# Transformer block with sliding-window attention on one core: dense matmuls in four column tiles, reordered score columns, an earlier output weight

## The chip, the cores and the metric

The kernel runs on one core of one Trainium2 chip. The metric is device time in microseconds (us) of one execution, the median over several runs. Names of engines: PE is TensorE (matmuls), DVE is VectorE, ACT is ScalarE, POOL is GpSimd, SP is SyncE, which here only issues DMA transfers.

## The reference

One layer with two branches on the same normalised input: attention with 32 heads of 20 dimensions over 2048 positions, each query seeing the last 256 keys, and a gated feed-forward part. All inputs are bf16.

```python
B, S, D = 1, 2048, 640          # F = 1536
xn = _layernorm(x)

# A: sliding-window attention, H = 32, Dh = 20, W = 256
q, k, v = split_heads(xn @ wqkv)
scores = einsum("bhqd,bhkd->bhqk", q, k) * Dh ** -0.5
mask = (idx[:, None] - idx[None, :] >= 0) & (idx[:, None] - idx[None, :] < W)
p = softmax(where(mask, scores, -1e9))
a = einsum("bhqk,bhkd->bhqd", p, v).reshape(B, S, D) @ wo

# B: gated feed-forward
b = (sigmoid(xn @ w_gate) * (xn @ w_up)) @ w_down

out = x + a + b
```

## The kernel before

The 2048 positions are cut into four chunks of 512 (`CW`), and a chunk into four blocks of 128. For each chunk there are these pieces of work.

- Layer norm of the chunk, and its transposed form `xnT`. Chunk 0 is transposed on PE (L276), chunks 1 to 3 by DMA transposes that SP issues (`turn_block`, L280).
- The q and k projections (`proj_block`, L296): 128 weight columns per matmul, taken from `wqkv` with a step of five, 512 columns of `xnT` streamed, five matmuls to sum over 640. Results go to bf16 on DVE (q) and ACT (k), to a scratch tensor in DRAM, and back as `qT` and `kT` (`spread`, L311) in a layout where each group of four heads stands at partitions 0, 32, 64 and 96.
- The v projection (`project_v`, L322): `xnT` as weights, 320 columns streamed. A column of 0.5 beside each head's v gives the softmax denominator.
- Gate and up (`g_gu`, L396 and L403): 24 times five matmuls of 512 columns per chunk. ACT takes tanh (L399), DVE makes `h` (L407).
- Down (`down`, L417) and the attention output (`add_wo`, L424), both into the same PSUM tile `y`, in halves of 320 columns; DVE adds x (L428), SP stores.

All these are called dense below. Their matmuls have 128 by 128 weights and fill the whole array.

The attention itself runs in steps over groups of four heads (`HG`); there are eight groups. A step (`wide_step`, `full_step`) computes 512 columns of scores per head, in units of 64 queries by 64 keys. Keys stand on the partitions in two halves (`hf`) of 64, and the four heads of a group use four row bands of the array: the score matmuls (L463) have weights of 20 rows by 64 columns. Chunk 0 has 16 wide steps; each later chunk has 16 wide steps (two per group) and four full steps (one per pair of groups, for blocks that no mask cuts). Each step writes the one PSUM tile `ps` (four banks, one buffer); ACT takes the exp into `pT` (L469, four buffers), in two instructions; POOL then clears what the mask forbids (L473): units on the diagonal (`diag`), the oldest unit (`oldest`), and a shifted copy of a unit that holds two half-forbidden ones (`late`), one instruction per place.

Two steps after a group's last step, PV for it is issued (`pv`, L494): for each head v's 32 columns as weights, at column band 32i of the array, so the four heads' matmuls go to four tiles of 32 columns. Its result `acc` is transposed and scaled on DVE into `oc`.

The order on PE is the program's order. The loop at the end walks over all 76 steps: PV of a group that is due, then the step's scores, then a share of dense work, pulled from a list of generators (`fill.add`, L643 to L661). Each generator yields its estimated PE time, and the loop spreads what is left up to the next due point evenly over the steps, by `units` (8 in every step). Transfers stand in the same list, so their place in it fixes their place in SP's queue, which is worked through in order. The last chunk's down and output are written out by hand after the loop, with the last PV among them.

The output weight `wo` has to be rearranged by heads: `turn_wo` (L220) copies it within DRAM to `wo_i`, and `load_wo` (L225) loads that. Its first use is in `out0`, the output of chunk 0. `load_wd` (L216) loads the down weights.

Of the kernel before, what the change touches and what calls it, by code (L numbers as in the profile page):

```python
# [9 lines left out]
P = 128  # L10
S = 2048
D = 640
# [3 lines left out]
DC = D // P  # L16
FC = F // P
CW = 512
NCH = S // CW
SBC = CW // P  # L20
HG = 4
# [3 lines left out]
HALF = 320  # L25
FS = 768
EPS = 1e-5
SCALE = DH ** -0.5
# [5 lines left out]
GE = mybir.AluOpType.is_ge  # L34
BF16 = mybir.dt.bfloat16
FP32 = mybir.dt.float32
EXP = mybir.ActivationFunctionType.Exp
# [5 lines left out]
U = 64  # L43
# [10 lines left out]

def wide_step(g, r, old):

    q = 2 * r  # L60
    scores = [(g, 0, r, q, 5, 0)]
    if old:
        scores += [(g, 1, r, q + 1, 5, 1), (g, 1, r - 2, q + 1, 1, 0), (g, 0, r + 2, q + 4, 2, 5),
                   (g, 1, r + 2, q + 5, 1, 6), (g, 1, r - 2, q, 1, 7), (g, 0, r - 2, q, 1, 7)]
        return dict(scores=scores, exps=[(0, 5, 0), (5, 3, 6)], late=[(0, 9), (6, 5)], diag=[0, 6],
                    oldest=[4, 8], pv=[(g, r, q, 6, 0), (g, r + 2, q + 4, 2, 6), (g, r - 2, q, 2, 8)],
                    units=8)

    scores += [(g, 1, r, q, 6, 0)]
    if r == 0:  # L70
        scores += [(g, 0, 2, 4, 3, 5), (g, 1, 2, 5, 2, 6)]
        last = [(g, 2, 4, 3, 6)]
    else:
        scores += [(g, 0, 3, 6, 2, 5), (g, 1, 3, 7, 1, 6), (g, 0, 2, 7, 1, 7), (g, 1, 2, 7, 1, 7)]
        last = [(g, 3, 6, 2, 6), (g, 2, 7, 1, 8)]
    return dict(scores=scores, exps=[(0, 5, 0), (5, 3, 6)], late=[(6, 5)], diag=[0, 6], oldest=[4],
                pv=[(g, r, q, 6, 0)] + last, units=8)


def full_step(gs):  # L80

    out = dict(scores=[], exps=[], late=[], diag=[], oldest=[], pv=[], units=8)
    for n, g in enumerate(gs):
        out["exps"].append((4 * n, 4, 4 * n))
        for r, q, col in ((-1, 0, 4 * n), (2, 6, 4 * n + 2)):
            out["scores"] += [(g, hf, r, q, 2, col) for hf in range(2)]
            out["pv"].append((g, r, q, 2, col))
    return out


def steps_of(c):
# [20 lines left out]
def kernel(  # L112
# [169 lines left out]
    def new_xnT(c):  # L282
        xnT[c] = xtp.tile([P, DC, CW], BF16, name="xnT")


    qk = {}
    vt = {}

    def proj_block(w, c, m):


        base = 0 if w == "q" else D
        ps = ps_d.tile([P, CW], FP32, name="pqk", tag="d")
        for d in range(DC):
            wt = wqkv[:, d, base:base + D].rearrange("p (k m) -> p m k", m=DC)
            nc.tensor.matmul(ps, lhsT=wt[:, m, :], rhs=xnT[c][:, d, :],  # L296
                             start=(d == 0), stop=(d == DC - 1))
        st = stp.tile([P, CW], BF16, name="st")
        if w == "q":
            nc.vector.tensor_copy(out=st, in_=ps)  # L300
        else:
            nc.scalar.copy(out=st, in_=ps)
        dst = scratch[w, c % 2].rearrange("(h j) s -> h j s", j=32)
        nc.sync.dma_start(out=dst[:, 4 * m:4 * m + 4, :], in_=st)
# [14 lines left out]
    def project_v(c, s, hf):  # L319
        ps = ps_d.tile([P, CW], FP32, name="pv", tag="d")  # L320
        for d in range(DC):
            nc.tensor.matmul(ps[:, 0:HALF], lhsT=xnT[c][:, d, s * P:(s + 1) * P],  # L322
                             rhs=wqkv[:, d, 2 * D + hf * HALF:2 * D + (hf + 1) * HALF],
                             start=(d == 0), stop=(d == DC - 1))
        return ps

    def copy_v(c, s, hf, ps, copy):
# [60 lines left out]
    def part(w, d, f):  # L388
        k, first = divmod(f * P, FS)
        return w[k][:, d, first:first + P]  # L390

    def g_gu(c, f0, f1):
        for f in range(f0, f1):
            pg = ps_d.tile([P, CW], FP32, name="pg", tag="d")
            for d in range(DC):
                nc.tensor.matmul(pg, lhsT=part(wg, d, f), rhs=xnT[c][:, d, :],  # L396
                                 start=(d == 0), stop=(d == DC - 1))
            th = tp.tile([P, CW], FP32, name="th")
            nc.scalar.activation(out=th, in_=pg, func=TANH, scale=0.5)  # L399
            yield 5 * MM  # L400
            pu = ps_d.tile([P, CW], FP32, name="pu", tag="d")
            for d in range(DC):
                nc.tensor.matmul(pu, lhsT=part(wu, d, f), rhs=xnT[c][:, d, :],  # L403
                                 start=(d == 0), stop=(d == DC - 1))
            h = hp.tile([P, CW], BF16, name="h")
            ht[c, f] = h
            nc.vector.scalar_tensor_tensor(out=h, in0=th, scalar=1.0, in1=pu, op0=ADD, op1=MULT)  # L407
            yield 5 * MM
# [5 lines left out]

    def down(c, s, y, cut):
        for f in range(FC):
            nc.tensor.matmul(y[:, 0:cut[1] - cut[0]], lhsT=ht[c, f][:, s * P:(s + 1) * P],  # L417
                             rhs=wd[:, f, cut[0]:cut[1]], start=(f == 0), stop=False)
            if f % 6 == 5:
                yield 6 * 136  # L420

    def add_wo(c, s, y, cut):
        for m in range(DC):
            nc.tensor.matmul(y[:, 0:cut[1] - cut[0]], lhsT=oc[c, m][:, s * P:(s + 1) * P],  # L424
                             rhs=wo[:, m, cut[0]:cut[1]], start=False, stop=(m == DC - 1))

    def add_x(c, s, y, cut, rows):
        nc.vector.scalar_tensor_tensor(  # L428
# [27 lines left out]
    def scores(c, step):  # L456
        pt = pp.tile([P, HG, PTW], BF16, name="pT")
        ps = ps_s.tile([P, HG, CW], FP32, name="ps")
        for g, hf, r, q, n, col in step["scores"]:
            kc, kb = divmod(c * SBC + r, SBC)  # L460
            key = kb * P + hf * U
            for i in range(HG):
                nc.tensor.matmul(  # L463
                    ps[hf * U:(hf + 1) * U, i, col * U:(col + n) * U],
                    lhsT=qk["k", kc][32 * i:32 * i + DH, g, key:key + U],
                    rhs=qk["q", c][32 * i:32 * i + DH, g, q * U:(q + n) * U],
                    start=True, stop=True)
        for col, n, to in step["exps"]:
            nc.scalar.activation(out=pt[:, :, to * U:(to + n) * U], in_=ps[:, :, col * U:(col + n) * U],  # L469
                                 func=EXP, scale=SCALE)  # L470

        def keep(out, in_, pattern, base, sign):
            nc.gpsimd.affine_select(out=out, in_=in_, pattern=[[0, HG], [sign, pattern]], compare_op=GE,  # L473
                                    fill=0.0, base=base, channel_multiplier=-sign)

        def cols(u, n):
            return pt[:, :, u * U:u * U + n]

        for a, b in step["late"]:
            keep(cols(b, U), cols(a, U), U, -1 - U, -1)  # L480
        for u in step["oldest"]:
            keep(cols(u, U), cols(u, U), U, -1, -1)
        for u in step["diag"]:
            keep(cols(u, P), cols(u, P), P, 0, 1)
        return pt

    def pv(c, g, parts):
# [76 lines left out]
    def mix(a, b, first, every=1, rest=True):  # L564

        for k, cost in enumerate(a):
            yield cost
            if k >= first and (k - first) % every == 0:
                yield next(b, 0)
        if rest:  # L570
            yield from b
# [66 lines left out]
    def later(load, *args):  # L638
        load(*args)
        yield 0  # L640

    norms2 = g_norms(2, True)
    fill.add("gu0", mix(g_gu(0, 0, 12), g_norms(1, True), 9), 12 * GU)  # L643
    fill.add("x2", later(load_x, 2), 0)
    fill.add("wd", later(load_wd), 0)
    fill.add("qk1", g_qk(1), 50 * MM)
    fill.add("v1", g_v(1), 40 * 136)
    fill.add("wo_i", later(turn_wo), 0)
    fill.add("gu1a", mix(g_gu(1, 0, 2), norms2, 0, 2, False), 2 * GU)
    fill.add("wo", later(load_wo), 0)  # L650
    fill.add("out0", mix(g_out(0), norms2, 0, 2), OUT)
    fill.add("x3", later(load_x, 3), 0)
    fill.add("qk2", g_qk(2), 50 * MM)
# [21 lines left out]
    for t, (c, k, step) in enumerate(todo):  # L675
        if k == 0 and c > 0:
            fill.until(f"qk{c}")
        if k == 2 and c > 0:
            fill.until(f"v{c}")
        for group in [x for x in ends if ends[x] == t - 2]:  # L680
            fill.flush()
            pv(*group, parts.pop(group))
            if group[1] == NG - 1:
                fill.shut.discard(f"out{group[0]}")
        made = (step, scores(c, step))
        for g in dict.fromkeys(piece[0] for piece in step["pv"]):
            parts.setdefault((c, g), []).append(made)
        last, label = next(x for x in cuts if t < x[0])
        credit += fill.left(label) * step["units"] / sum(x[2]["units"] for x in todo[t:last])
        credit = fill.pull(credit)  # L690
    fill.pull(10 ** 9)
    fill.flush()
# [61 lines left out]
```

## Time and profile before

| | |
|---|---|
| median of 13 runs | 317.22 us (316.85 to 319.74) |
| profiled execution | 317.37 us, of which the profile's span is 315.4 |
| PE busy | 306.9 us (97%) |
| ACT busy | 198.1 us (63%) |
| POOL busy | 178.9 us (57%) |
| DVE busy | 154.3 us (49%) |
| granted PE clock | full, in all slices |
| DMA | 33.05 MB, mean 105 GB/s, busiest in the first 80 us |

The profile is one execution. A row of its groups names the source line, the engine, the operation, the tiles (written from read) and the shapes, then the busy time, the mean duration of one in ns, and the idle time of the engine just before such instructions with what ended it. Matmuls overlap, so their mean duration is longer than the distance from one start to the next, and a busy PE need not be streaming at its full rate. The timeline merges neighbouring instructions of a kind and gives the start and length of the whole.

### The profile page before, as it was taken

The page shows a single profiled execution, that of the slowest core. Times are in us where ns is not written, and L with a number is a line of the kernel's source. Part 1 is how long each engine was busy: PE and PEld are TensorE (multiplying, and loading weights), DVE is VectorE, ACT ScalarE, POOL GpSimd, SP SyncE. Part 2 cuts the span into 40 slices and gives each one's busy share as a digit, 9 for nine tenths or more (in the row PEclk, how much of TensorE's full clock was granted, in tenths as well). Part 3 has the DMA queues.
Part 4 walks back from the last instruction along what each step waited for, and adds up shares of the span by engine and source line. Part 5 has one row for each costly group of instructions (what it writes and reads, how often), then busy time and mean ns, then how long its engine had stood idle before and what let it go on. Part 6 is the DMA issues. An engine that isn't in the chain of part 4 may idle for free.

```text
span 315.4 us, 10274 instructions
## 1 busy us (share of the span) xinstructions
PE 306.9 (97%) x4370; PEld 175.4 (56%) x4410; DVE 154.3 (49%) x313; ACT 198.1 (63%) x255; POOL 178.9 (57%) x417
## 2 busy tenths in 40 slices
PE   8999999999989999999999999999999999999996
PEld 3654444456556655544466655544456664444674
DVE  3531486654854563347753542444552433563234
ACT  5723887788845458677744457776765657878200
POOL 3000487667768548565975647476365767676300
PEclk9999999999999999999999999999999999999999
DMA  7985958836754255510036025600000010000002
GB/s 255 375 302 191 323 194 133 295 94 208 257 94 61 52 173 176 148 51 2 0 43 88 23 89 144 224 3 2 3 3 23 25 42 3 2 2 2 0 2 83
DMA packets 34572, 33.05 MB, mean 105 GB/s; under 512 B 9920, under 2 KB 33984, under 8 KB 34496
## 3 DMA queue, kind: packets, MB, share of 16 engines
q1 hardware_dynamic: 34096, 32.14, 34.6%
q8 instruction: 34, 0.56, 0.7%
q10 hardware_dynamic: 432, 0.28, 0.3%
q14 instruction: 10, 0.08, 0.1%
HBM read 21.00 MB, written 10.26 MB: 99 GB/s over the span
## 4 chain that ended last, share of the span: by engine, by line
PE 88%; DMA 6%; ACT 3%; issue 2%; SPq 1%; DVE 0%; ACTq 0%
PE pg L396 16%; PE pu L403 16%; PE y L417 14%; PE pqk L296 13%; PE ps L463 8%; PE acc L494 7%; PE y L424 6%; PE pv L322 5%; DMA wo_i<-in_A_wo_dram 2%; PE d L417 2%; DMA sk<-st 2%; ACT pT L469 1%; DMA wo<-wo_i 1%; DMA xc<-in_A_x_dram 1%; SPq L220 1%
## 5 line engine op out<-in xcount | busy, mean ns | idle before, releaser
L473 POOL TENSOR_SCALAR_AFFINE_SELECT pT<-pT 128x256 bf16<-128x256 bf16 (+1 forms) x352 | 164.8, 502 | 114.8 <-ACT pT L469 114.5
L469 ACT ACTIVATE pT<-ps 128x1280 bf16<-128x1280 f32 (+2 forms) x152 | 147.4, 1023 | 64.8 <-PE ps L463 61.7
L407 DVE SCALAR_TENSOR_TENSOR h<-th,pu 128x512 bf16<-128x512 f32 x48 | 32.8, 683 | 56.6 <-PE pu L403 33.2
L396 PE MATMUL pg<-xnT,wg 128*128 128x512 bf16 x222 | 58.7, 380 | 0.9
L403 PE MATMUL pu<-xnT,wu 128*128 128x512 bf16 x228 | 58.0, 380 | 1.1 <-issue 0.6
L417 PE MATMUL y<-wd,h 128*128 128x320 bf16 (+1 forms) x348 | 50.2, 297 | 0.0
L296 PE MATMUL pqk<-xnT,wqkv 128*128 128x512 bf16 x190 | 45.5, 382 | 0.5
L417 PEld LDWEIGHTS <-h 128*128 128x128 bf16 x396 | 36.7, 98 | 14.1 <-issue 0.2
L504 DVE STREAM_TRANSPOSE t<-acc 128x512 f32<-128x512 f32 x32 | 22.8, 712 | 33.5 <-PE acc L494 33.3
L399 ACT ACTIVATE th<-pg 128x512 f32<-128x512 f32 x48 | 28.8, 601 | 14.4 <-PE pg L396 7.7
L403 PEld LDWEIGHTS <-wu 128*128 128x128 bf16 x240 | 22.0, 98 | 25.4 <-issue 0.6
L396 PEld LDWEIGHTS <-wg 128*128 128x128 bf16 x240 | 22.0, 98 | 24.8 <-issue 0.4
L463 PEld LDWEIGHTS <-kT 20*64 20x64 bf16 x2048 | 22.1, 104 | 19.6 <-issue 16.2
L463 PE MATMUL ps<-qT,kT 20*64 20x64 bf16 (+3 forms) x2048 | 32.8, 232 | 0.1
L296 PEld LDWEIGHTS <-wqkv 128*128 128x128 bf16 x200 | 22.5, 119 | 17.9 <-issue 0.6
L428 DVE SCALAR_TENSOR_TENSOR xn<-y,xc 128x320 bf16<-128x320 f32 (+1 forms) x29 | 13.9, 483 | 31.0 <-PE y L424 30.9
L494 PE MATMUL acc<-pT,v 128*32 128x128 bf16 (+2 forms) x928 | 25.7, 250 | 0.0
L494 PEld LDWEIGHTS <-v 128*32 128x32 bf16 x928 | 16.9, 97 | 15.3 <-issue 11.0
L322 PE MATMUL pv<-wqkv,xnT 128*128 128x320 bf16 x160 | 23.8, 300 | 0.0
L424 PE MATMUL y<-wo,oc 128*128 128x320 bf16 (+1 forms) x145 | 21.6, 297 | 1.5 <-DMA wo<-wo_i 1.5
L516 DVE TENSOR_TENSOR on<-t,rec 128x320 bf16<-128x320 f32 (+4 forms) x48 | 20.9, 435 | 1.1
L424 PEld LDWEIGHTS <-oc 128*128 128x128 bf16 x165 | 15.5, 98 | 7.6 <-issue 1.8
(49 smaller groups left out, 149.8 us busy)
## 6 DMA issues: line engine op xcount, KB each, us to landing
qT<-sq SPq DMA_DIRECT2D x3, 1024.0 KB, 5.8
sq<-st SPq DMA_DIRECT2D x20, 128.0 KB, 3.2
sk<-st SPq DMA_DIRECT2D x20, 128.0 KB, 3.4
out_dram<-xn SPq DMA_DIRECT2D x15, 160.0 KB, 1.8
kT<-sk SPq DMA_DIRECT2D x3, 768.0 KB, 5.5
wg<-in_B_w_gate_dram SPq DMA_DIRECT2D x2, 960.0 KB, 7.4
wu<-in_B_w_up_dram SPq DMA_DIRECT2D x2, 960.0 KB, 12.1
xc<-in_A_x_dram SPq DMA_DIRECT2D x3, 640.0 KB
```

Of the source, the lines that this page charges most:

```text
L296: nc.tensor.matmul(ps, lhsT=wt[:, m, :], rhs=xnT[c][:, d, :], start=(d == 0), stop=(d == DC - 1))
L322: nc.tensor.matmul(ps[:, 0:HALF], lhsT=xnT[c][:, d, s * P:(s + 1) * P], rhs=wqkv[:, d, 2 * D + hf * HALF:2 * D + (hf + 1) * HALF], start=( ...
L396: nc.tensor.matmul(pg, lhsT=part(wg, d, f), rhs=xnT[c][:, d, :], start=(d == 0), stop=(d == DC - 1))
L399: nc.scalar.activation(out=th, in_=pg, func=TANH, scale=0.5)
L403: nc.tensor.matmul(pu, lhsT=part(wu, d, f), rhs=xnT[c][:, d, :], start=(d == 0), stop=(d == DC - 1))
L407: nc.vector.scalar_tensor_tensor(out=h, in0=th, scalar=1.0, in1=pu, op0=ADD, op1=MULT)
L417: nc.tensor.matmul(y[:, 0:cut[1] - cut[0]], lhsT=ht[c, f][:, s * P:(s + 1) * P], rhs=wd[:, f, cut[0]:cut[1]], start=(f == 0), stop=False)
L424: nc.tensor.matmul(y[:, 0:cut[1] - cut[0]], lhsT=oc[c, m][:, s * P:(s + 1) * P], rhs=wo[:, m, cut[0]:cut[1]], start=False, stop=(m == DC - 1))
L463: nc.tensor.matmul(ps[hf * U:(hf + 1) * U, i, col * U:(col + n) * U], lhsT=qk["k", kc][32 * i:32 * i + DH, g, key:key + U], rhs=qk["q", c] ...
L469: nc.scalar.activation(out=pt[:, :, to * U:(to + n) * U], in_=ps[:, :, col * U:(col + n) * U], func=EXP, scale=SCALE)
L473: nc.gpsimd.affine_select(out=out, in_=in_, pattern=[[0, HG], [sign, pattern]], compare_op=GE, fill=0.0, base=base, channel_multiplier=-sign)
L494: nc.tensor.matmul(acc[32 * i:32 * i + 32, q * U:(q + n) * U], lhsT=v[:, h * VW:h * VW + 32], rhs=pt[:, i, col * U:(col + n) * U], start=( ...
```

## The change

1. **Score columns.** In the wide steps of chunks 1 to 3 the pieces are rearranged so that a head needs six score matmuls instead of seven, and the units that one mask treats alike stand five units apart (`SPAN`). Every step then has one exp over all 512 columns of a head, and each of the three masks is one instruction over both of its places. `late` units now go to `pT` columns 8 and 9 (9 in chunk 0), behind those that the exp writes. PV has to take these units on their own, so its pieces are more and smaller. Chunk 0's steps keep their score pieces.
2. **Transfers.** `load_wd` moves from behind gate and up of chunk 0 into it, after four of its twelve parts; `turn_wo` moves from behind chunk 1's v projection to before its q and k projections; `load_wo` moves one place ahead. The order of dense work on PE stays.
3. **Dense matmuls.** A helper `dense` issues each dense matmul as four, with 32 weight columns each, into the four 32-partition bands of the output. Chunk 0's v projection and the transposes stay as they are.
4. The share of fill per step is spread by steps, not by `units`, which were equal.

The instruction lists of the two programs count so: score matmuls 2048 before and 1856 after, PV matmuls 928 and 1376, exps 152 and 76, masks 352 and 192, PE instructions in all 8,822 and 17,500.

```diff
+SPAN = 5
 def wide_step(g, r, old):
     q = 2 * r
-    scores = [(g, 0, r, q, 5, 0)]
     if old:
-        scores += [(g, 1, r, q + 1, 5, 1), (g, 1, r - 2, q + 1, 1, 0), (g, 0, r + 2, q + 4, 2, 5),
-                   (g, 1, r + 2, q + 5, 1, 6), (g, 1, r - 2, q, 1, 7), (g, 0, r - 2, q, 1, 7)]
-        return dict(scores=scores, exps=[(0, 5, 0), (5, 3, 6)], late=[(0, 9), (6, 5)], diag=[0, 6],
-                    oldest=[4, 8], pv=[(g, r, q, 6, 0), (g, r + 2, q + 4, 2, 6), (g, r - 2, q, 2, 8)],
-                    units=8)
+        return dict(scores=[(g, 0, r, q, 5, 1), (g, 1, r, q + 1, 5, 2), (g, 0, r + 2, q + 4, 2, 6),
+                            (g, 1, r - 2, q, 2, 0), (g, 0, r - 2, q, 1, 0), (g, 1, r + 2, q + 5, 1, 7)],
+                    late=(1, 8, 2), diag=1, oldest=(0, 2),
+                    pv=[(g, r, q, 5, 1), (g, r + 2, q + 4, 2, 6), (g, r, q + 5, 1, 9),
+                        (g, r - 2, q, 1, 0), (g, r - 2, q + 1, 1, 8)])
+    scores = [(g, 0, r, q, 5, 0), (g, 1, r, q, 6, 0)]
...
+    return dict(scores=scores, late=(5, 9, 1), diag=0, oldest=(4, 1),
+                pv=[(g, r, q, 5, 0), (g, r, q + 5, 1, 9)] + last)
...
+    def dense(out, lhsT, rhs, start, stop):
+        for j in range(0, P, 32):
+            nc.tensor.matmul(out[j:j + 32], lhsT=lhsT[:, j:j + 32], rhs=rhs, start=start, stop=stop)
...
 # proj_block; likewise in g_gu (pg, pu), down and add_wo
-            nc.tensor.matmul(ps, lhsT=wt[:, m, :], rhs=xnT[c][:, d, :],
-                             start=(d == 0), stop=(d == DC - 1))
+            dense(ps, wt[:, m, :], xnT[c][:, d, :], d == 0, d == DC - 1)
 # project_v
-            nc.tensor.matmul(ps[:, 0:HALF], ...)
+            (dense if c else nc.tensor.matmul)(ps[:, 0:HALF], ...)
...
 # scores
-        for col, n, to in step["exps"]:
-            nc.scalar.activation(out=pt[:, :, to * U:(to + n) * U], in_=ps[:, :, col * U:(col + n) * U],
-                                 func=EXP, scale=SCALE)
+        nc.scalar.activation(out=pt[:, :, 0:CW], in_=ps, func=EXP, scale=SCALE)
+        def keep(out, in_, n, width, base, sign):
+            nc.gpsimd.affine_select(out=out, in_=in_, pattern=[[0, HG], [0, n], [sign, width]],
+                                    compare_op=GE, fill=0.0, base=base, channel_multiplier=-sign)
+        def spans(u, n, units):
+            a, b = divmod(u, SPAN)
+            two = pt.rearrange("p h (a b) -> p h a b", a=2)
+            return two[:, :, a:a + n, b * U:(b + units) * U]
+        if "late" in step:
+            src, to, n = step["late"]
+            keep(pt[:, :, to * U:(to + n) * U].rearrange("p h (n u) -> p h n u", u=U),
+                 spans(src, n, 1), n, U, -1 - U, -1)
+            u, n = step["oldest"]
+            keep(spans(u, n, 1), spans(u, n, 1), n, U, -1, -1)
+            keep(spans(step["diag"], 2, 2), spans(step["diag"], 2, 2), 2, P, 0, 1)
...
-    fill.add("gu0", mix(g_gu(0, 0, 12), g_norms(1, True), 9), 12 * GU)
+    fill.add("gu0a", g_gu(0, 0, 4), 4 * GU)
+    fill.add("wd", later(load_wd), 0)
+    fill.add("gu0b", mix(g_gu(0, 4, 12), g_norms(1, True), 1), 8 * GU)
     fill.add("x2", later(load_x, 2), 0)
-    fill.add("wd", later(load_wd), 0)
+    fill.add("wo_i", later(turn_wo), 0)
     fill.add("qk1", g_qk(1), 50 * MM)
     fill.add("v1", g_v(1), 40 * 136)
-    fill.add("wo_i", later(turn_wo), 0)
+    fill.add("wo", later(load_wo), 0)
     fill.add("gu1a", mix(g_gu(1, 0, 2), norms2, 0, 2, False), 2 * GU)
-    fill.add("wo", later(load_wo), 0)
     fill.add("out0", mix(g_out(0), norms2, 0, 2), OUT)
...
-        credit += fill.left(label) * step["units"] / sum(x[2]["units"] for x in todo[t:last])
+        credit += fill.left(label) / (last - t)
```

More of the change, by code (lines that the diff above doesn't have):

```diff
@@ L44 @@
 PTW = 10 * U
+SPAN = 5
 def wide_step(g, r, old):
     q = 2 * r
-    scores = [(g, 0, r, q, 5, 0)]
     if old:
-        scores += [(g, 1, r, q + 1, 5, 1), (g, 1, r - 2, q + 1, 1, 0), (g, 0, r + 2, q + 4, 2, 5),
-                   (g, 1, r + 2, q + 5, 1, 6), (g, 1, r - 2, q, 1, 7), (g, 0, r - 2, q, 1, 7)]
-        return dict(scores=scores, exps=[(0, 5, 0), (5, 3, 6)], late=[(0, 9), (6, 5)], diag=[0, 6],
-                    oldest=[4, 8], pv=[(g, r, q, 6, 0), (g, r + 2, q + 4, 2, 6), (g, r - 2, q, 2, 8)],
-                    units=8)
-    scores += [(g, 1, r, q, 6, 0)]
+        return dict(scores=[(g, 0, r, q, 5, 1), (g, 1, r, q + 1, 5, 2), (g, 0, r + 2, q + 4, 2, 6),
[4 more added lines that the diff above has]
+    scores = [(g, 0, r, q, 5, 0), (g, 1, r, q, 6, 0)]
     if r == 0:
         scores += [(g, 0, 2, 4, 3, 5), (g, 1, 2, 5, 2, 6)]
-        last = [(g, 2, 4, 3, 6)]
+        last = [(g, 2, 4, 3, 5)]
     else:
         scores += [(g, 0, 3, 6, 2, 5), (g, 1, 3, 7, 1, 6), (g, 0, 2, 7, 1, 7), (g, 1, 2, 7, 1, 7)]
-        last = [(g, 3, 6, 2, 6), (g, 2, 7, 1, 8)]
-    return dict(scores=scores, exps=[(0, 5, 0), (5, 3, 6)], late=[(6, 5)], diag=[0, 6], oldest=[4],
-                pv=[(g, r, q, 6, 0)] + last, units=8)
+        last = [(g, 3, 6, 2, 5), (g, 2, 7, 1, 7)]
+    return dict(scores=scores, late=(5, 9, 1), diag=0, oldest=(4, 1),
+                pv=[(g, r, q, 5, 0), (g, r, q + 5, 1, 9)] + last)
 def full_step(gs):
[L82 to L88, printed above, removed]
+    pieces = [(g, r, q, 2, 4 * n + col) for n, g in enumerate(gs) for r, q, col in ((-1, 0, 0), (2, 6, 2))]
+    return dict(scores=[(g, hf, *rest) for g, *rest in pieces for hf in range(2)], pv=pieces)
 def steps_of(c):
@@ L321, in project_v @@
         for d in range(DC):
-            nc.tensor.matmul(ps[:, 0:HALF], lhsT=xnT[c][:, d, s * P:(s + 1) * P],
-                             rhs=wqkv[:, d, 2 * D + hf * HALF:2 * D + (hf + 1) * HALF],
-                             start=(d == 0), stop=(d == DC - 1))
+            (dense if c else nc.tensor.matmul)(
+                ps[:, 0:HALF], lhsT=xnT[c][:, d, s * P:(s + 1) * P],
+                rhs=wqkv[:, d, 2 * D + hf * HALF:2 * D + (hf + 1) * HALF],
+                start=(d == 0), stop=(d == DC - 1))
         return ps
@@ L395, in g_gu @@
             for d in range(DC):
-                nc.tensor.matmul(pg, lhsT=part(wg, d, f), rhs=xnT[c][:, d, :],
-                                 start=(d == 0), stop=(d == DC - 1))
+                dense(pg, part(wg, d, f), xnT[c][:, d, :], d == 0, d == DC - 1)
             th = tp.tile([P, CW], FP32, name="th")
@@ L402, in g_gu @@
             for d in range(DC):
-                nc.tensor.matmul(pu, lhsT=part(wu, d, f), rhs=xnT[c][:, d, :],
-                                 start=(d == 0), stop=(d == DC - 1))
+                dense(pu, part(wu, d, f), xnT[c][:, d, :], d == 0, d == DC - 1)
             h = hp.tile([P, CW], BF16, name="h")
@@ L416, in down @@
         for f in range(FC):
-            nc.tensor.matmul(y[:, 0:cut[1] - cut[0]], lhsT=ht[c, f][:, s * P:(s + 1) * P],
-                             rhs=wd[:, f, cut[0]:cut[1]], start=(f == 0), stop=False)
+            dense(y[:, 0:cut[1] - cut[0]], ht[c, f][:, s * P:(s + 1) * P],
+                  wd[:, f, cut[0]:cut[1]], f == 0, False)
             if f % 6 == 5:
@@ L423, in add_wo @@
         for m in range(DC):
-            nc.tensor.matmul(y[:, 0:cut[1] - cut[0]], lhsT=oc[c, m][:, s * P:(s + 1) * P],
-                             rhs=wo[:, m, cut[0]:cut[1]], start=False, stop=(m == DC - 1))
+            dense(y[:, 0:cut[1] - cut[0]], oc[c, m][:, s * P:(s + 1) * P],
+                  wo[:, m, cut[0]:cut[1]], False, m == DC - 1)
     def add_x(c, s, y, cut, rows):
@@ L467, in scores @@
                     start=True, stop=True)
-        for col, n, to in step["exps"]:
-            nc.scalar.activation(out=pt[:, :, to * U:(to + n) * U], in_=ps[:, :, col * U:(col + n) * U],
-                                 func=EXP, scale=SCALE)
[L472 to L484, printed above, removed]
+        nc.scalar.activation(out=pt[:, :, 0:CW], in_=ps, func=EXP, scale=SCALE)
[13 more added lines that the diff above has]
+            keep(spans(step["diag"], 2, 2), spans(step["diag"], 2, 2), 2, P, 0, 1)
         return pt
```

## The prediction

> **What bounds the kernel now.** I read the busy shares first, then the waits, then the tensor engine's own timeline.
>
> ```profile
> span 315.4 us, 10274 instructions
> ...
> PE 306.9 (97%) x4370; PEld 175.4 (56%) x4410; DVE 154.3 (49%) x313; ACT 198.1 (63%) x255; POOL 178.9 (57%) x417
> ```
>
> TensorE (PE) is busy from end to end; the others stand at half to two thirds. The waits (engine and line, released by, us in total, times, longest) agree: the long ones are other engines waiting for PE or for each other, and PE's one sizeable wait is for `wo`.
>
> ```profile
> POOL pT L473 <- ACT pT L469: 114.5, 87, 30.5
> ACT pT L469 <- PE ps L463: 61.7, 54, 3.3
> ...
> PE y L424 <- DMA wo<-wo_i: 1.5, 1, 1.5
> ```
>
> The chain of waits has DMA for 6%, but its stretch at 72 to 90 us lies beside a PE that the timeline shows working, so there only the 1.5 us count. "Busy" is not "streaming", so I look at where one kind of matmul follows another (start, us, shape of weights, shape of moving data):
>
> ```profile
> 205.15 1.24 PE L403 MATMUL pu<-xnT,wu 128*128 128x512 bf16 x5
> 206.32 0.84 PE L494 MATMUL acc<-pT,v 128*32 128x384 bf16 x32
> 207.10 0.43 PE L463 MATMUL ps<-qT,kT 20*64 20x320 bf16 x28
> 207.46 1.25 PE L396 MATMUL pg<-xnT,wg 128*128 128x512 bf16 x4
> ```
>
> Inside a run of dense matmuls the starts are 216 ns apart, so five take 1.08 us and PV could begin at 206.23; it begins at 206.32. I took this over all starts in the trace: start to start, less columns / 2.4 per ns. Inside dense runs the remainder is 2.5 to 3 ns. Wherever the weights' shape changes it is 96 ns (middle value; 94 to 97 covers nearly all): dense to scores 45 times, PV to scores 31, scores to dense 76, dense to PV 32, PV to dense once. That is 185 switches, 17.8 us.
>
> PV shows what four 32-column matmuls cost. The four heads' matmuls start 2 to 4 ns apart, and the next four follow as if the first had been one full-width matmul: 163 ns later at 384 columns, 83 at 192, 56 at 128.
>
> [...] at PV's 128 columns each load starts 2 ns after a matmul and the next matmul 54 ns after that, so a load takes no more than 54. [...]
>
> **The change part by part.** The profiled execution took 317.37 us: the span of 315.4 and 1.97 around it. The median is 317.22, 0.15 less.
>
> *Dense in column tiles.* Dense and PV then have one shape, so 33 switches go (32 into PV, one out of it in the tail); one appears, where chunk 0 goes from transposes and full-width v projections to its q projection. Net 32 x (96 - 2.5) = **-3.0 us**, all on PE and so all on the path. Switches to and from scores stay; scores to 32-column tiles is not in the trace, and I give it the 96 that all five other kinds show. The pitch of four: 216 ns at 512 columns and 136 at 320, by the PV row, so 0[...]. The strided q/k weights (119 ns reported against 98) are the weak spot: now the first pitch after a switch is 34 ns too long there, eight times, so I allow -0.3 to +0.5.
>
> *PV.* Two pieces per wide step and group appear in chunks 1 to 3 (48 steps, 96 groups of four), and one per step in chunk 0 (16): 112 groups of four, 448 matmuls. The columns streamed stay the same (384+128+128 becomes 320+128+64+64+64), so the cost is 2.5 ns each, **+0.3 us**. But 160 of the groups are now 64 wide, and no row here shows a 64-wide PV group followed by another. In the scores, 64 after 64 comes at 29 to 31 ns with 20x64 weights; I take that. If the weight load sets 56 ns, as at 128 columns, it is 27 x 160 = +4.3 us more. [...]
>
> *Scores.* 48 steps lose four matmuls each, and both key halves get 320+128+64. The halves run side by side; the longer one (320+64+64+64) loses one gap of some 4 ns: **-0.2 us**. The instruction lists also show that the first weight load of 68 of the 76 steps waits for PE itself, and none does after. Dense to scores, where most of these waits stand, costs the same 96 as dense to PV, which has none, so the wait ends within the switch: a gain is excluded, and taking it away can cost nothing.
>
> *Exps and masks.* The rows (busy us, mean ns):
>
> ```profile
> L473 POOL TENSOR_SCALAR_AFFINE_SELECT pT<-pT 128x256 bf16<-128x256 bf16 x224 | 89.3, 424 | 114.8 <-ACT pT L469 114.5
> L469 ACT ACTIVATE pT<-ps 128x1280 bf16<-128x1280 f32 x64 | 79.2, 1238 | 55.8 <-PE ps L463 52.9 <-POOL pT L473 2.6
> L473 POOL TENSOR_SCALAR_AFFINE_SELECT pT<-pT 128x512 bf16<-128x512 bf16 x128 | 78.8, 639 | 0.0
> ...
> L469 ACT ACTIVATE pT<-ps 128x768 bf16<-128x768 f32 x64 | 51.7, 808 | 0.0
> ```
>
> ACT: 808 at 768 and 1238 at 1280 give 163 + 0.84 per element, so 1883 at 2048. 76 of these are 143.1 us, against 154.2 for the 152 old ones: -11.1. POOL: 424 and 639 give 209 + 0.84, so 1069 at 1024. 64 x 1069 + 96 x 639 + 32 x 424 = 143 against 168: -25. Worth **0**: PE is the bound. The cover to keep is that the single `ps` buffer is free before the next scores. An exp pair now takes 1.94 us and starts only after the step's last score; one of 1.88 ends sooner. Only one score step, at 286 us, began late beyond its switch, by 0.2. Masks now start after the whole exp, not its first part, but exp and masks together take 1.88 + 0.64 + 0.64 + 1.07 = 4.2 us against about 4.6, and PV reads them two steps (some 7 us) later.
>
> *Queues.* On SP (issue start, us):
>
> ```profile
> 44.55 6.97 SPq L280 DMA_TRANSPOSE xnT<-xn  x4
> 51.58 0.58 SPq L159 DMA_DIRECT2D xc<-in_A_x_dram  x1
> 52.21 0.49 SPq L216 DMA_DIRECT2D wd<-in_B_w_down_dram  x1
> ...
> 77.85 2.81 SPq L220 DMA_DIRECT2D wo_i<-in_A_wo_dram  x4
> 83.42 3.35 SPq L225 DMA_DIRECT2D wo<-wo_i  x4
> ```
>
> PE waited from its last `y` matmul at 88.25 to 90.09, 1.84 us where 0.14 was due; `oc` had been ready since 87.1. After the change wo_i's four issues come right after `x` (near 52 us) and wo's four stay behind kT's, at 77.9 but with nothing to wait for: issued by 79.5, behind kT (landed 83.1), landed near 85.6, needed near 87.2. **-1.7 us**; late next is oc, which is ready. The `wd` load moves ahead of the four transposes on SP, to about 36.7 us, when SP is idle. The second half of the gate and up weights keeps the DMA engines full to 43 us; wd's 1.97 MB at the 0.37 MB/us seen at 54 to 60 takes 5.3, so to 48.3. The transposes' first packets moved at 46, so these lose some 2 us, but the last one waits for DVE until 50.3 and lands near 55, with q/k for chunk 1 due at 56.8. Cost 0, with 1.5 us of cover; at worst +2. wo_i stands in front of the q/k stores, where wd stood: 2.8 us of issues, done by 55, before the first store at 58.8. POOL and ACT queues issue no moved DMA.
>
> Sum: -3.0 + 0.3 - 0.2 - 1.7 = -4.6, so 312.8 against the profiled execution and **312.6 us** against the median.
>
> **The rivals.**
>
> *64-wide PV groups bound by their weight loads.* For it: no 64-wide sequence is on record, and loads may take up to 54 ns. Against: scores at 29 to 31. Time 312.6 + 4.3 = 316.9; half of it, 314.8.
>
> *A transfer comes late* (wd before the transposes, or kT when PE arrives 0.8 us sooner at chunk 1). For: the covers are 1.5 us or less. Against: the DMA gap at 42 to 46 us. Time 313.5 to 315.5.
>
> *Instructions come too slowly: slower.* PE's list grows from 8,822 to 17,500. A 512-column group of four is eight instructions in 216 ns, 27 ns each; a 320-column group is eight in 136, **17 ns each**, for long stretches (681 groups: v, down and wo). The trace shows 115 PE instructions in the densest 1 us, 221 in 4, 374 in 8. [...] The gain is gone from 17.9 ns on (4.6 us / 681 / 8 = 0.85 above 17). For: nothing on record is as dense for long. Against: bursts of 72 in 0.5 us (7 ns each) show no seam, and instruction fetches (16 KB, 256 instructions) take about 1 us each where one would be due every 4.4.
>
> *It does not do what it says:* the switch costs 96 by itself even within one shape of weights, if some other property matters. PV's own stream speaks against it. Then only wo counts: 315.7.
>
> **How the numbers follow.** Working as summed: 0.66. Weight loads bind: 0.10. Late transfer: 0.06. No switch saved: 0.03. Too slow a supply: 0.15, 318.5 to 331. The likeliest gives **312.6 us**. Its own bounds (q/k loads, a switch cost of scores to 32-column tiles that is 20 ns off either way over 76, and half of PV's doubt) span 310.9 to 314.8; the range reaches through the late and load-bound cases to **316.6**, leaving out the slow supply and a little at each end. Under 0.3% (1 us) a measurement of this kernel can't tell from no change: faster **0.82**, same **0.03**, slower **0.15**.
>
> **What would show it.** Right: starts of dense matmuls in fours at 216 and 136 ns, no 96 ns at PV's start, still 96 around scores, no wait of `y` for `wo`, ACT and POOL shorter with PE's share unchanged. Wrong: 320-column groups over 140 ns apart; 64-wide PV groups near 56; a gap before chunk 1's q/k projection at 56 us, or before its first scores at 80.

## The result and the profile after

The changed kernel takes 324.71 us (median of 11 runs), the kernel before 317.22. The ratio is 1.0216, 95% interval 1.0191 to 1.0241: 2.2% slower, where 1.5% faster was forecast. Three executions of the changed kernel, of 327.2 to 329.4 us, lie over 1.5% above its fastest; they count as slow and are left out of the ratio. The profiled execution is the one of 324.71 us, with a span of 323.0.

From the page after, busy time, share and instructions of each engine, and the DMA queue that brings instructions (packets, MB, share of 16 engines):

```profile
span 323.0 us, 18737 instructions
...
PE 311.2 (96%) x8749; PEld 196.4 (61%) x8749; DVE 157.7 (49%) x313; ACT 193.3 (60%) x179; POOL 159.1 (49%) x257
...
q8 instruction: 68, 1.11, 1.4%
```

The same queue on the page before:

```profile
q8 instruction: 34, 0.56, 0.7%
```

PE is still the bound, ACT and POOL are relieved as forecast, and twice as many instruction blocks of 16 KB are fetched. In the waits after there is no wait of `y` for `wo`. New ones stand in their place, PE waiting for "issue", that is, for nothing that another engine or a data transfer of the program would release:

```profile
PEld L284 <- issue: 12.0, 24, 2.7
...
PE pv L284 <- issue: 2.6, 2, 1.7
...
PE pu L284 <- issue: 2.2, 1, 2.2
...
PE acc L494 <- issue: 1.7, 1, 1.7
```

The PE timeline after shows one of them (start, us, shapes, count; in brackets the idle time before and what ended it):

```profile
50.94 1.26 PE L284 MATMUL pu<-xnT,wu 128*32 128x512 bf16 x18
54.42 0.47 PE L284 MATMUL pu<-xnT,wu 128*32 128x512 bf16 x2 [2.23 <-issue]
54.43 2.60 PE L284 MATMUL pg<-xnT,wg 128*32 128x512 bf16 x20
```

PE stops after 18 of the 20 column matmuls of one accumulation. The last two read the same tiles as the 18 before them, so no data is late; the 19th pair of instructions (weight load and matmul) is. The twenty that follow take 2.60 us instead of some 1.25: after the idle time the granted clock was lower, as the stretch from 54 to 56 us shows (length, busy us with counts for PE, weight loads, DVE, ACT, POOL, then the granted clock, DMA share, GB/s):

```profile
54.00:56.00 2.00, 1.58 (x20) 0.68 (x24) 0.69 (x1) 0.00 (x0) 1.44 (x2) 0.65 1.31 210
```

All the larger stops are at one kind of place. Counting PE's weight loads and matmuls from the start, the last one before each stop is number 1470, 1726, 3002, 3514, 4792, 5558, 10676 and 13234: the distances from the first are 1, 6, 8, 13, 16, 36 and 46 times 256, to within 12. (They fall short by about as much as PE's list holds waits for semaphores, which this count leaves out: 11 are recorded from 60 to 252 us. Counted with these, the distances are exact multiples.) A packet of 16 KB thus holds 256 instructions, called a block below, and the 68 packets for 17,500 instructions (257 each) agree. No packet in the trace began to move more than 1.0 us before PE's first instruction of the block before it.

The packets' times show why the block was late. In a quiet stretch (240 to 272 us, 25 GB/s) the packet of a block begins to move 0.5 to 1.1 us after PE's first instruction of the block before it, and moves for about 1 us. At each stop PE goes on 1.1 to 1.5 us after the packet has landed. That makes 3 to 4 us in all. For the stops at 46, 52, 80, 90 and 207 us the packet began to move 3.9, 4.9, 2.5, 4.4 and 3.3 us after PE's first instruction of the block before, beside 250 to 340 GB/s at the last three. From one block to the next it is mostly 7 to 10 us in the kernel before (8.2 in the middle), and 3.4 to 5.6 after (4.2). From 16 us on, gaps of over 60 ns beyond the distance that is due from one start to the next (columns / 2.4 + 2.5 ns, or + 96 at a change of shape) sum to 9.6 us, and the slow clock adds 1.5.

### The profile page after: what moved, and what is told of

It reads as the page before. It is cut to its first block, busy times and chain, and to the rows that moved or that the text cites. A ratio compares the mean times of both kernels' runs of the same rounds, so it can differ in the third digit from the quotient of the medians.

```text
span 323.0 us, 18737 instructions
## 1 busy us (share of the span) xinstructions
PE 311.2 (96%) x8749; PEld 196.4 (61%) x8749; DVE 157.7 (49%) x313; ACT 193.3 (60%) x179; POOL 159.1 (49%) x257
## 4 chain that ended last, share of the span: by engine, by line
PE 96%; issue 2%; DVE 0%
PE y L284 21%; PE pg L284 17%; PE pu L284 17%; PE pqk L284 14%; PE ps L462 9%; PE acc L494 6%; PE pv L284 5%; PE d L284 2%; PE pv L322 2%; PE pwarm L236 2%; PE acc L284 0%; PE pt L272 0%; DVE xnT L273 0%; DVE xn L427 0%; DVE st L165 0%
## 5 line engine op out<-in xcount | busy, mean ns | idle before, releaser
L470 POOL TENSOR_SCALAR_AFFINE_SELECT pT<-pT 128x512 bf16<-128x512 bf16 (+2 forms) x192 | 144.9, 785 | 142.4 <-ACT pT L467 142.2
L467 ACT ACTIVATE pT<-ps 128x2048 bf16<-128x2048 f32 x76 | 142.7, 1877 | 65.3 <-PE ps L462 60.4
L284 PE MATMUL pu<-xnT,wu 128*32 128x512 bf16 x960 | 62.2, 383 | 2.2 <-issue 2.2
L284 PE MATMUL pg<-xnT,wg 128*32 128x512 bf16 x960 | 62.3, 385 | 0.8 <-issue 0.7
L284 PE MATMUL y<-wd,h 128*32 128x320 bf16 (+1 forms) x1392 | 50.7, 297 | 0.0
L284 PEld LDWEIGHTS <-h 128*32 128x32 bf16 x1584 | 41.2, 97 | 10.1 <-issue 0.2
L284 PE MATMUL pqk<-xnT,wqkv 128*32 128x512 bf16 x800 | 46.6, 381 | 0.1
L284 PEld LDWEIGHTS <-wu 128*32 128x32 bf16 x960 | 25.5, 98 | 26.4 <-issue 4.9
L462 PE MATMUL ps<-qT,kT 20*64 20x128 bf16 (+4 forms) x1856 | 33.1, 239 | 0.2 <-issue 0.2
L494 PE MATMUL acc<-pT,v 128*32 128x64 bf16 (+3 forms) x1376 | 26.7, 222 | 1.7 <-issue 1.7
```

The costliest lines, as they stand in the source:

```text
L284: nc.tensor.matmul(out[j:j + 32], lhsT=lhsT[:, j:j + 32], rhs=rhs, start=start, stop=stop)
L462: nc.tensor.matmul(ps[hf * U:(hf + 1) * U, i, col * U:(col + n) * U], lhsT=qk["k", kc][32 * i:32 * i + DH, g, key:key + U], rhs=qk["q", c] ...
L467: nc.scalar.activation(out=pt[:, :, 0:CW], in_=ps, func=EXP, scale=SCALE)
L494: nc.tensor.matmul(acc[32 * i:32 * i + 32, q * U:(q + n) * U], lhsT=v[:, h * VW:h * VW + 32], rhs=pt[:, i, col * U:(col + n) * U], start=( ...
```

## Experiments

The theory, A, is this: PE's instruction list comes in blocks of 256, a block's fetch is delayed beside other DMA traffic, and column tiles make a block last half as long, so the delay is no longer covered.

**All but the tiles.** In `dense`:

```diff
-        for j in range(0, P, 32):
-            nc.tensor.matmul(out[j:j + 32], lhsT=lhsT[:, j:j + 32], rhs=rhs, start=start, stop=stop)
+        nc.tensor.matmul(out, lhsT=lhsT, rhs=rhs, start=start, stop=stop)
```

> All of the change but the column tiles: dense matmuls go out whole again. Theory A (PE waits for blocks of 256 instructions whose fetch comes late beside other DMA traffic, and needs them twice as often when the list is twice as long): no wait for instructions is left, PV +0.3, wo -1.7, scores -0.2, so 315.6 us (315.2 to 316.3). Rival B (the moved transfers, wd ahead of the transposes, cause the gaps): the gaps near 47 and 52 us stay, 319 us or more. Rival C (PV's many small pieces are what costs): over 317.

Measured 315.73 us, ratio 0.9936 (0.9914 to 0.9959). No stop for a late block is left; the two largest gaps are 0.3 us, at scores and at `wo`'s first matmul, both with waits for data. So scores, masks, PV's small pieces and the transfers together are worth what the prediction gave them, and B and C fall.

**The transfers alone.** The kernel before with the list's lines for `wd`, `wo_i` and `wo` moved as in the change (`fill.add` only).

> The kernel before with nothing but the moved transfers (wd, wo_i and wo earlier). The prediction's term stands by itself: wo's wait of 1.7 us goes and nothing else changes, 315.5 us (315.2 to 316.2). If the early wd delays the transposes, or the stretch ahead of the output matmuls is held by something else next, 316.5 to 317.5.

Measured 315.85 us, ratio 0.9951 (0.9938 to 0.9963), and 1.5 us off the profiled span. All of the untiled kernel's gain, within the intervals, is wo's wait; the score columns, masks and PV pieces together are worth nothing measurable.

**The tiles alone.** The kernel before, with `dense` in the same places as in the change.

> The kernel before with nothing but the column tiles. A: no 96 ns ahead of PV (-3.0 us), but waits at every 256th PE instruction of some 8 to 12 us in all, as after the change: 321 to 326 us. B: the transfers stand where they stood, so no gaps: 314.2 us.

Measured 325.18 us, ratio 1.0230 (1.0204 to 1.0255). The loss comes with the tiles alone, without the moved transfers. The stops at block ends now fall mainly at 66, 82, 91 and 135 us (1.5, 0.7, 1.6 and 1.4 us), since the transfers stand elsewhere. Two more stops of this profile lie away from block ends and are for data:

```profile
PE ps L467 <- DMA kT<-sk: 2.1, 1, 2.1
...
PE y L289 <- DMA wo<-wo_i: 1.3, 1, 1.3
```

The second is the old wait for `wo`, at 96 us. The first, at 31 us, was followed by 1.4 us of slow clock. The changed kernel's profile has no such wait, but a later profile of the same stretch of program has it too (1.7 us, the first kernel under "Load added" below), so it varies from execution to execution. About 6 of the 11 us that this profile lost are thus late blocks.

**As many instructions without tiles.**

```diff
-        for j in range(0, P, 32):
-            nc.tensor.matmul(out[j:j + 32], lhsT=lhsT[:, j:j + 32], rhs=rhs, start=start, stop=stop)
+        n = rhs.shape[-1] // 4
+        for j in range(4):
+            nc.tensor.matmul(out[:, j * n:(j + 1) * n], lhsT=lhsT, rhs=rhs[:, j * n:(j + 1) * n], ...)
```

> As after the change, but each dense matmul is cut in four along the streamed columns (4 x 128 or 4 x 80) with the full 128x128 weights: the same number of PE instructions, no column tiles, the switches ahead of PV back. Without waits for instructions it costs 7.5 ns more for each of 1361 dense groups, 10.2 us, so 326 us if the weight loads keep up. A: waits at every 256th instruction here too, 3 to 10 us, so 329 to 336. D (column tiles themselves, not their number, cause the gaps): no such waits, 326.

Measured 336.25 us, ratio 1.0560 (1.0519 to 1.0602), a hair over A's range. Its PE timeline at the place of the first fence:

```profile
51.53 1.18 PE L285 MATMUL pu<-xnT,wu 128*128 128x128 bf16 x18
54.40 0.29 PE L285 MATMUL pu<-xnT,wu 128*128 128x128 bf16 x2 [1.68 <-issue]
54.52 1.28 PE L285 MATMUL pg<-xnT,wg 128*128 128x128 bf16 x20
```

With full-width weights PE stops after the same 18 of 20 matmuls. Gaps counted as above sum to 7.8 us, which with the 326 worked out for no waits makes 333.8, against 334.32 for the profiled execution. D, column tiles themselves, falls: it is the number of instructions.

**Load added where it was quiet.** Five copies of a 1.97 MB tensor within DRAM during chunk 2's gate and up, to the kernel after and to the kernel before.

```diff
+    junk = tc.dram_tile([D, F], BF16, name="junk")
+    def more_load(gen, every):
+        for k, cost in enumerate(gen):
+            if k % every == 0:
+                nc.sync.dma_start(out=junk.rearrange(...), in_=B_w_gate.rearrange(...))
+            yield cost
...
-    fill.add("gu2", g_gu(2, 0, 12), 12 * GU)
+    fill.add("gu2", more_load(g_gu(2, 0, 12), 5), 12 * GU)
```

> After the change, with five copies of the gate weights within DRAM (1.97 MB each, result unused) issued during chunk 2's gate and up, a stretch of some 35 us from 220 us on that had little DMA and no wait over 0.1 us. A: new waits at every 256th instruction there, several of 0.5 to 2 us each, 3 to 10 us more than after the change: 328 to 335. E: no new waits, 324.7.

> The kernel before with the same five copies at the same place. A: a block of 256 instructions lasts 7 to 9 us here and covers the late fetch, so no waits for instructions: 317.2 us, within 0.5. A general effect of DMA load on PE would show here as well.

Measured 333.13 us after (ratio to the kernel before 1.0478, 1.0431 to 1.0525), 8.4 more than the changed kernel, and 317.31 before (1.0000, 0.9980 to 1.0021). The timeline of the former, in a stretch whose stops without the load were 0.2 us at most:

```profile
248.00 0.37 PE L462 MATMUL ps<-qT,kT 20*64 20x128 bf16 x24
249.84 0.26 PE L462 MATMUL ps<-qT,kT 20*64 20x128 bf16 x8 [1.47 <-issue]
...
252.68 1.27 PE L284 MATMUL y<-wd,h 128*32 128x320 bf16 x32
256.31 0.99 PE L284 MATMUL y<-wd,h 128*32 128x320 bf16 x12 [2.37 <-issue]
```

And two stretches under that load, first of the kernel after, then of the kernel before (columns as above):

```profile
226.00:231.00 5.00, 4.06 (x100) 1.90 (x96) 1.42 (x3) 3.09 (x4) 2.33 (x3) 1.00 0.78 301
...
252.00:257.00 5.00, 2.63 (x80) 1.69 (x76) 0.75 (x2) 1.99 (x2) 2.13 (x3) 0.90 0.87 329
```

```profile
225.00:230.00 5.00, 5.00 (x105) 2.69 (x105) 2.52 (x5) 3.38 (x4) 2.73 (x6) 1.00 0.97 363
235.00:240.00 5.00, 5.00 (x116) 3.13 (x114) 2.86 (x5) 2.38 (x3) 3.34 (x9) 1.00 0.69 265
```

PE loses 0.9 and 2.4 of 5 us in one and nothing in the other, at like traffic (301 and 329 GB/s against 363 and 265). The packets were late in both: up to 3.9 us after PE's first instruction of the block before (at 250 us) in the one, and 3.7 us (at 225 us) in the other, where that block lasted 9.2 us. This is the cleanest proof of A: load makes blocks late, and late blocks stop PE only where blocks are short. From 215 to 262 us the gaps sum to 5.6 us, against 0.3 in the changed kernel. Elsewhere that profile differs both ways, as one execution does from another: the stop near 55 us was longer (3.5 us against 2.4), the slow clock cost 2.3 us against 1.5, and PE waited 2.0 us for `kT` and `wu` before 45 us; the stops at 80 and 207 us were shorter (0.3 and 0.1 us against 1.1 and 1.8).

**Load taken away.**

```diff
 # proj_block, after the cast to st
+        if c:
+            return
 # spread
+        if c:
+            qk[w, c] = qk[w, 0]
+            return
```

> After the change, less DMA: chunks 1 to 3 use chunk 0's q and k, so their stores to scratch and their loads are left out (the projections and casts still run). A: instruction blocks come in time from about 65 us on, so the waits at 80, 90 and 207 us and the small ones (some 5 us together) go, those at 46 to 58 stay: 318 to 320 us. Rival E (PE decodes too slowly for 17 ns per instruction, whatever DMA does): all waits stay, 324 us.

This kernel leaves out the stores and loads of q and k for chunks 1 to 3 and uses those of chunk 0 instead, so it does not compute the layer. Measured 323.55 us (321.87 to 325.13), ratio 1.0191 (1.0137 to 1.0245): outside A's 318 to 320. The profile has the places right and the size wrong. The stops at 80, 90 and 207 us are gone, and gaps after 65 us fall from 6.1 to 1.6 us. But those before 65 us, where the traffic is as it was, grew from 3.5 to 4.2, and stops of 0.4 to 0.5 us at block ends are left at 109, 256 and 264 us, the one at 256 with no other packet on any DMA queue from 252.7 us on: the block before it had 3.3 us of work, and the new one needed 3.7 (1.15 us until its packet began to move, 1.3 to move, 1.3 until PE went on). So blocks that are too short cost something by themselves, and traffic adds to it. E asked for all stops to stay, and falls. The profiled execution is the fastest of the four, 321.87 us, and its sum comes close: 312.8, 5.9 of gaps, 1.5 of slow clock and 1.2 of waits for the first layer norm make 321.4. What the other executions lost beyond that, 1.7 us at the median, no profile shows.

**Tiles of 64 columns.** Two matmuls in place of four (`range(0, P, 64)`), so about half the added instructions.

> After the change with two 64-column tiles in place of four of 32: 12,056 PE instructions, and the switch ahead of PV is back, since 64-column tiles aren't PV's shape. A: blocks last some 6.5 us, so the waits shrink to 0 to 3 us: 315.7 to 318.7. D (column tiles themselves cause the gaps): some 10 us remain, 325.

Measured 318.71 us, ratio 1.0023 (1.0006 to 1.0041), at the upper end of A's range. One stop at a block's end is large (0.9 us beyond the switch, at 200 us). Of the rest over the untiled kernel, 1.3 us is the first group after a switch from scores: 14 ns longer than with full weights, and 36 ns at q and k, 76 times in all. D would have needed 325.

**Tiles only where they save a switch.** A flag, set per step, lets `dense` tile only between a step's scores and the next step's PV, and in the tail; the second version leaves out chunk 1's v projection and first gate and up.

```diff
+        if not tiled:
+            nc.tensor.matmul(out, lhsT=lhsT, rhs=rhs, start=start, stop=stop)
+            return
 # in the loop over steps, after the scores
+        tiled.clear()
+        if any(ends[x] == t - 1 for x in ends) or t == len(todo) - 1:
+            tiled.add(t)
```

> As after the change, but only those dense matmuls are tiled that lie between a step's scores and the next step's PV, and those of the tail; the others go out whole. 13,048 PE instructions. All 33 switches at PV are still saved (-3.0). A: a block of 256 lasts some 6 us on average, so few late fetches: waits 0 to 4 us, 312.8 to 316.8. C: over 317.

> As the kernel that is tiled only ahead of PV, but the stretches of chunk 1's v projection and first gate and up parts, beside which the q/k loads and wo run, go out whole: 12,868 PE instructions, two or three switches kept (+0.2 to +0.3). A: the 2 us wait for instructions at 86 us, which that kernel's profile shows, goes or moves, so 312.9 to 313.9 with less spread between executions.

Measured 313.41 us, ratio 0.9856 (0.9831 to 0.9880), and 313.18 us, ratio 0.9863 (0.9845 to 0.9880). Both beat both kernels. The profile of the first has one stop at a block's end (1.85 us at 86 us, in an execution of 315.37 us); the second's waits have none of that kind. The second's page:

```profile
span 311.9 us, 14076 instructions
...
PE 303.2 (97%) x6404; PEld 185.4 (59%) x6433; DVE 156.9 (50%) x313; ACT 193.1 (62%) x179; POOL 159.6 (51%) x257
```

By the ratios the two gain 2.5 and 2.3 us on the untiled kernel, of the 3.0 that the switches are worth.

## Why the prediction was wrong

*The steps that held.* The switch ahead of PV is gone in the changed kernel. From its timeline:

```profile
88.68 1.25 PE L284 MATMUL pu<-xnT,wu 128*32 128x512 bf16 x20
89.75 0.64 PE L494 MATMUL acc<-pT,v 128*32 128x320 bf16 x24
```

Five groups from 88.68 end their streaming at 89.76 and PV starts at once. Scores to 32-column tiles costs 91 ns, taken as 96. Groups of four come at 216 and 136 ns. PV's 64-wide groups come at 29 ns, so that rival is out. wo's wait was put at 1.7 and measured at 1.4 to 1.5. All the signs that the prediction named for being right appeared, so they could not tell its outcome from this one. The exp was put at 1883 ns and the masks at 1069 and 639:

```profile
L467 ACT ACTIVATE pT<-ps 128x2048 bf16<-128x2048 f32 x76 | 142.7, 1877 | 65.3 <-PE ps L462 60.4 <-POOL pT L470 4.6
L470 POOL TENSOR_SCALAR_AFFINE_SELECT pT<-pT 128x1024 bf16<-128x1024 bf16 x64 | 70.6, 1103 | 0.0
L470 POOL TENSOR_SCALAR_AFFINE_SELECT pT<-pT 128x512 bf16<-128x512 bf16 x96 | 62.9, 679 | 92.2 <-ACT pT L467 92.1
```

The masks cost 34 and 40 ns more each, hidden as forecast: the untiled and the transfers-alone kernels differ by 0.1 us in their medians and 0.5 us by their ratios, within the intervals.

*The step that failed.* It is the sentence against the last rival: "instruction fetches (16 KB, 256 instructions) take about 1 us each where one would be due every 4.4". The 1 us is how long the packet moves. The time that counts runs from PE's first instruction of the previous block to the first of the new one: 3 to 4 us when DMA is quiet, and 7.3 from 47.1 to 54.4 us. Set against 4.4 us (312.6 us for 17,500 instructions make it 4.6), that is no cover, so a term put at nothing was worth +11.1 us (9.6 of stops, 1.5 of slow clock). With it, 312.8 becomes 323.9 for the profiled execution's 324.71; some 0.8 us stay unassigned, of which 0.2 to 0.3 is `wo`'s term.

*The rival on the slow side* named the instruction supply and gave it 0.15, with the wrong mechanism: a steady rate per instruction, which would have stretched every 320-column group. That its times, 318.5 to 331 us, take in the measured 324.71 is luck; its upper end was the author's estimate, and no trace or run here shows a supply as slow as that. The groups kept their 136 ns, and from 250.6 us on PE ran 637 instructions in 8 us (13 ns each) with one stop of 0.2 us, at a block's end. The supply is fast within a block and late between blocks. The packets' times, which would have shown this, are in the trace of before: the one for the block used from 65.6 us began to move 4.1 us after PE's first instruction of the block before it.

*The prediction's care for transfers* went to the data that they carry, and asked only whether `xnT`, `wo` or `kT` come late. That the same 16 DMA engines carry the program (q8, 1.4% of their time on the page after) was not asked.

## What to carry to other kernels

An edit that multiplies the instructions of a busy engine can have a price in instruction blocks, here 11.1 us for twice the instructions: take the instructions per block from the fetch packets (here 256), work out how long a block will last (4.2 us after, 8.2 before), and set that against the time from the start on one block to the first use of the next (3 to 4 us in quiet stretches here, 7.3 at the largest stop), in the stretch with the heaviest transfers. If the block gets shorter than that, apply the edit only where it pays (here the dense work between scores and PV, 313.41 us) so that blocks with and without it mix. Here the stops whose operands were all ready, and that recurred at multiples of 256 in instruction count, were the program arriving late.

## What the runs showed of the hardware

- A change of the weights' shape cost 96 ns between any two of the full, 20x64 and 128x32 shapes (91 from scores to 128x32), and a group of four column tiles, with its four weight loads, took as long as one full matmul: 216 ns at 512 columns and 136 at 320. PV's groups came at 29 ns at 64 columns.
- A stop of 2.4 us of PE (2.23 of them idle) was followed by 3.4 us at a granted clock of 0.5 (54.6 to 58.0 us), in which matmuls of 512 columns started 427 ns apart, twice their distance. So this late block of instructions cost 1.5 us more than its own length. In all profiles here, such a stretch began within 1.1 us of the end of each of the six idle times of PE of 2.1 to 3.3 us, and of none of those of up to 1.85 us.
- Those executions of the changed kernel on which the ratio rests spread from 322.3 to 326.7 us, and the untiled kernel's from 315.4 to 316.3. That the wait for a block depends on the traffic of the moment would explain it; no run shows it execution by execution.
